# Moving more of an FFT and ReGLU kernel's mirror products from TensorE to GpSimd, with new buffers, 480 mirror columns and an fp32 row

## The chip, the cores and the metric

One core of a Trainium2 chip. The metric is the device time of one execution in microseconds (us); the profile's span is some 1.8 us shorter. Engines are named as in the profile: PE (TensorE matmul), PEld (its weight loads), DVE (VectorE), ACT (ScalarE), POOL (GpSimd), SP (SyncE, which here only issues DMAs). In a profile line, L465 is line 465 of the kernel that ran; the changed kernel has other line numbers.

## The reference

```python
X = np.fft.fft(x, axis=1)              # x: (8, 3008, 256)
X = np.fft.fft(X, axis=2)
y = X.real.reshape(24064, 256)
gate = np.maximum(y @ w_gate, 0.0)     # w_gate, w_val: (256, 1536)
val = y @ w_val
out = (gate * val) @ w_out             # w_out: (1536, 256)
```

The kernel folds the transform along the model axis into the weights. The real part of a 2D transform is symmetric: the output row k and its mirror row -k come from the same two arrays (called p and q in the kernel), once as gate = relu(P + Q), once as relu(P - Q); the value likewise.

## The kernel before

There are eight images. Each has three blocks of 12 steps, so there are 288 steps, numbered t; a step is one block and one of 12 slices of the hidden width. Each step makes an h tile of 128x2x512: half 0 is the direct product gate times value, half 1 the mirror product. A second matmul, 12 steps later, multiplies h by w_out.

PE's results go to PSUM (the memory that matmuls write and add into), bank by bank. Other intermediate tiles come from rings: a ring of five buffers gives a sixth tile no place until the first has been read for the last time.

The mirror's *value* can be had in two ways:

- **Not split:** PE adds a third matmul into the value's PSUM bank (with the weights wm, which are -2 times ws), and DVE multiplies it by the mirrored gate.
- **Split:** DVE keeps E (the even part: the value after its first matmul, plus a correction by the Nyquist row nb), later makes 2E - V of it, and POOL multiplies. PE is spared one matmul; DVE and POOL get more work.

```python
    gp = ctx.enter_context(tc.tile_pool(name="gp", bufs=5, space=SB))
    ep = ctx.enter_context(tc.tile_pool(name="ep", bufs=3, space=SB))
    op = ctx.enter_context(tc.tile_pool(name="op", bufs=3, space=SB))

    def split(t):
        return NBLK * NF + 8 <= t < len(steps) and t % 3 != 2      # from step 44 on

    def gate(t):
        ...                                          # two matmuls into G
        nc.scalar.activation(e["gs"][:], e["G"][:], ACTF.Relu)     # gs: a gp buffer

    def mirror_gate(t):
        nc.tensor.matmul(e["G"][:], lhsT=wm[0]..., rhs=pqt[b, blk][:, 1, :], start=False, ...)
        e["gm"] = gp.tile([128, 512], F32, tag="gs", name="gm")    # gm: the same ring as gs
        nc.scalar.activation(e["gm"][:], e["G"][:], ACTF.Relu)

    def even(t):
        e["E"] = ep.tile([128, 512], F32, tag="e", name="E")
        nc.vector.scalar_tensor_tensor(e["E"][:], nbt[b, blk][:], af[:, f:f + 1], e["V"][:],
                                       op0=ALU.mult, op1=ALU.add)

    def mirror_value(t):
        if split(t):
            nc.vector.scalar_tensor_tensor(e["E"][:], e["E"][:], 2.0, e["V"][:], op0=ALU.mult, op1=ALU.subtract)
            mirror_h(t, nc.gpsimd, e["E"])           # h half 1 = gm * E, on POOL
        else:
            nc.tensor.matmul(e["V"][:], lhsT=wm[1]..., rhs=pqt[b, blk][:, 1, :], start=False, ...)
            mirror_h(t, nc.vector, e["V"])
```

The PE order of a step matters: gate(t), then the *second* value matmul of step t-1 (value(t-1, 1)), then half of the output matmuls, then the first value matmul of step t and E of it on DVE. So the second value matmul of t-1 waits until DVE has read the bank for E(t-1).

POOL has a second duty. In 22 steps of an image it **folds** the input of the image after the next (sums and differences of rows, in place): one operation at the end of each step, behind that step's mirror product, on a queue that keeps its order.

```python
            at(t0 + tl, load_x, b + 2, nc.sync)                       # from image 2: step 7
            at(t0 + tf, lambda b=b: folds.append(fold(b + 2, nc.gpsimd)))  # from image 2: step 13
    ...
        for k in range(2 if t < NBLK * NF + 8 else 1):
            while folds and next(folds[0], folds) is folds:
                folds.pop(0)
```

One part of a fold's input (the tile xl) is loaded through SP, the other (xh) by an indirect DMA that POOL itself issues, from the same queue:

```python
    def load_x(b, q):
        ...                                          # xl: two DMAs on q, which is SP
        nc.gpsimd.indirect_dma_start(out=xh[:]..., ...)
```

Five folds (of images 3 to 7, run during images 1 to 5) fall where steps are split; the fold of image 2 ends there.

## Time and profile before

| | before |
|---|---|
| time, median | 690.5 us (690.15 to 691.46, 4 runs) |
| PE, DVE, ACT, POOL busy | 95%, 74%, 63%, 62% |
| matmul pitch, start to start | 0.215 us at 512 columns, 0.109 us at 256 |
| PE work of a steady image by these pitches | 76.1 us, of 79 to 80 us that it takes |
| one fold | 46.9 us for 22 steps |

The first part of the page of the kernel before (busy time of each engine), and from its second part the rows of PE and POOL in 40 equal slices of the span, in tenths:

```profile
PE 653.0 (95%) x4297; PEld 419.5 (61%) x4297; DVE 508.5 (74%) x800; ACT 436.2 (63%) x811; POOL 424.1 (62%) x398
...
PE   2799999999999999999999999999899999999996
...
POOL 1219801984998499747995399846996343344331
```

The share of POOL says little: 62% is a mean of stretches of 9 (folds) and of 3 to 5. The stretch view over one fold of the kernel before, with busy us and number of instructions by engine, shows it:

```profile
core 0: us, PE busy (x) PEld busy (x) DVE busy (x) ACT busy (x) POOL busy (x), PEclk, DMA share, GB/s
237.40:284.30 46.90, 44.81 (x308) 28.79 (x306) 36.58 (x57) 29.87 (x56) 46.74 (x43) 1.00 0.25 72
```

POOL is busy for 46.74 of 46.90 us. Inside, the timeline of POOL (start, duration, line, what it is) has no gap between the mirror products (L465) and the fold:

```profile
256.61 1.27 POOL L465 TENSOR_TENSOR h<-gm,E 128x512 bf16<-128x512 f32 x1
257.84 1.80 POOL L100 TENSOR_TENSOR xl<-xl,xh 94x768 f32<-94x768 f32 x1
259.61 1.26 POOL L465 TENSOR_TENSOR h<-gm,E 128x512 bf16<-128x512 f32 x1
260.84 0.98 POOL L101 TENSOR_TENSOR eo<-xc 94x381 bf16<-94x381 f32 x1
261.78 0.20 POOL L103 CAST eo<-xl 94x6 bf16<-94x6 f32 x1
261.93 0.98 POOL L104 TENSOR_TENSOR eo<-xl 94x381 bf16<-94x381 f32 x1
262.88 1.26 POOL L465 TENSOR_TENSOR h<-gm,E 128x512 bf16<-128x512 f32 x1
```

A mirror product takes 1.23 us of POOL's time (start to the next start), an operation of the fold 0.15 to 1.8. The waits view (who waited for whom: total us, times, longest) shows how that reaches PE. ACT's next gs wants a buffer of the shared ring that POOL's late product still reads, and PE's mirror-gate matmul (L439) waits for gs:

```profile
POOL h L465 <- DVE E L473: 166.0, 87, 3.8
...
ACT gs L434 <- POOL h L465: 12.6, 16, 1.2
...
PE G L439 <- ACT gs L434: 9.5, 14, 1.0
```

The first line is the other side: outside folds POOL sits idle, waiting for work.

### The profile page before, as it was taken

The page shows a single profiled execution, that of the slowest core. Times are in us where ns is not written, and L with a number is a line of the kernel's source. Part 1 is how long each engine was busy: PE and PEld are TensorE (multiplying, and loading weights), DVE is VectorE, ACT ScalarE, POOL GpSimd, SP SyncE. Part 2 cuts the span into 40 slices and gives each one's busy share as a digit, 9 for nine tenths or more (in the row PEclk, how much of TensorE's full clock was granted, in tenths as well). Part 3 has the DMA queues.
Part 4 walks back from the last instruction along what each step waited for, and adds up shares of the span by engine and source line. Part 5 has one row for each costly group of instructions (what it writes and reads, how often), then busy time and mean ns, then how long its engine had stood idle before and what let it go on. Part 6 is the DMA issues. An engine that isn't in the chain of part 4 may idle for free.

```text
span 688.8 us, 12467 instructions
## 1 busy us (share of the span) xinstructions
PE 653.0 (95%) x4297; PEld 419.5 (61%) x4297; DVE 508.5 (74%) x800; ACT 436.2 (63%) x811; POOL 424.1 (62%) x398
## 2 busy tenths in 40 slices
PE   2799999999999999999999999999899999999996
PEld 1444665666566656666666666666566666666665
DVE  8447555578778778787778878778788788888881
ACT  5555665667676766676666757676666856665561
POOL 1219801984998499747995399846996343344331
PEclk9999999999999999999999999999999999999999
DMA  9692257239314822176112931258211241211213
GB/s 235 216 218 37 63 143 173 48 97 203 113 50 122 199 79 74 40 167 203 38 42 67 234 105 41 74 124 216 59 48 38 60 123 38 78 32 36 54 31 90
DMA packets 31843, 70.74 MB, mean 103 GB/s; under 512 B 4410, under 2 KB 21426, under 8 KB 29394
## 3 DMA queue, kind: packets, MB, share of 16 engines
q1 hardware_dynamic: 29444, 58.16, 31.6%
q0 software_dynamic: 2336, 11.80, 8.4%
q8 instruction: 33, 0.54, 0.4%
q14 instruction: 30, 0.25, 0.1%
HBM read 39.77 MB, written 30.96 MB: 103 GB/s over the span
## 4 chain that ended last, share of the span: by engine, by line
PE 61%; POOL 18%; DMA 10%; issue 5%; DVE 2%; ACT 2%; SPq 1%; POOLq 0%; DVEq 0%
PE po L494 24%; PE V L451 7%; POOL h L465 7%; PE G L439 6%; PE G L432 6%; PE G L433 6%; PE V L449 6%; DMA xl<-in_x_dram 5%; POOL xl L100 4%; POOL xc L99 4%; PE V L476 3%; DMA xh<-in_x_dram,ix 3%; DMA xh<-in_x_dram 2%; PE psw L251 2%; POOL eo L101 2%
## 5 line engine op out<-in xcount | busy, mean ns | idle before, releaser
L494 PE MATMUL po<-wo,h 128*128 128x256 bf16 x2304 | 323.2, 272 | 0.0
L465 POOL TENSOR_TENSOR h<-gm,E 128x512 bf16<-128x512 f32 x162 | 205.9, 1271 | 166.6 <-DVE E L473 166.0
L494 PEld LDWEIGHTS <-h 128*128 128x128 bf16 x2304 | 222.8, 98 | 83.5 <-issue 7.5
L442 ACT ACTIVATE gm<-G 128x512 f32<-128x512 f32 x288 | 172.5, 599 | 129.8 <-PE G L439 128.2
L453 DVE TENSOR_TENSOR h<-gs,V 128x512 bf16<-128x512 f32 x288 | 190.7, 685 | 58.7 <-PE V L451 47.1
L434 ACT ACTIVATE gs<-G 128x512 f32<-128x512 f32 x288 | 171.6, 596 | 15.0 <-POOL h L465 12.6
L465 DVE TENSOR_TENSOR h<-gm,V 128x512 bf16<-128x512 f32 x126 | 86.7, 688 | 85.6 <-ACT gm L442 60.8
L459 DVE SCALAR_TENSOR_TENSOR E<-nb,af,V 128x512 f32<-128x512 bf16 x162 | 120.8, 746 | 6.6 <-PE V L449 6.1
L439 PE MATMUL G<-pq,wm_107 128*128 128x512 bf16 x288 | 109.1, 379 | 9.9 <-ACT gs L434 9.5
L473 DVE SCALAR_TENSOR_TENSOR E<-E,V 128x512 f32<-128x512 f32 x162 | 110.2, 680 | 0.0
L432 PE MATMUL G<-pq,wc_103 128*128 128x512 bf16 x288 | 109.1, 379 | 1.0 <-ACT pq L206 1.0
L449 PE MATMUL V<-pq,wc_104 128*128 128x512 bf16 x288 | 109.1, 379 | 0.0
L433 PE MATMUL G<-pq,ws_105 128*128 128x512 bf16 x288 | 109.1, 379 | 0.0
L451 PE MATMUL V<-pq,ws_106 128*128 128x512 bf16 x288 | 109.0, 379 | 0.0
L497 ACT COPY os<-po 128x512 f32<-128x512 f32 x96 | 56.2, 585 | 67.9 <-PE po L494 67.9
L99 POOL TENSOR_TENSOR xc<-xl,xh 94x768 f32<-94x768 f32 x35 | 63.4, 1811 | 50.0 <-DMA xl<-in_x_dram 34.1
L100 POOL TENSOR_TENSOR xl<-xl,xh 94x768 f32<-94x768 f32 x35 | 63.4, 1812 | 1.6
L433 PEld LDWEIGHTS <-ws_105 128*128 128x128 bf16 x288 | 28.1, 98 | 35.0 <-issue 1.1
L451 PEld LDWEIGHTS <-ws_106 128*128 128x128 bf16 x288 | 28.1, 98 | 34.2 <-DVE ws_106 L256 0.4
L476 PE MATMUL V<-pq,wm_108 128*128 128x512 bf16 x126 | 47.7, 379 | 0.3
L432 PEld LDWEIGHTS <-wc_103 128*128 128x128 bf16 x288 | 28.1, 98 | 18.6 <-issue 15.6
L449 PEld LDWEIGHTS <-wc_104 128*128 128x128 bf16 x288 | 28.2, 98 | 17.6 <-issue 1.3
(361 smaller groups left out, 385.5 us busy)
## 6 DMA issues: line engine op xcount, KB each, us to landing
out_dram<-os SPq DMA_DIRECT2D x176, 128.0 KB
xl<-in_x_dram SPq DMA_DIRECT2D x7, 1360.0 KB
nb<-Nd SPq DMA_DIRECT2D x24, 128.0 KB
xl<-in_x_dram SPq DMA_DIRECT2D x7, 238.0 KB
xl<-in_x_dram SPq DMA_DIRECT2D x2, 768.0 KB
xh<-in_x_dram SPq DMA_DIRECT2D x2, 768.0 KB
wst<-in_moe_w_gate_dram SPq DMA_DIRECT2D x6, 256.0 KB
wst<-in_moe_w_val_dram SPq DMA_DIRECT2D x6, 256.0 KB
```

What stands on the lines that cost most here:

```text
L432: nc.tensor.matmul(e["G"][:], lhsT=wc[0][:, fs], rhs=pq[:, 0, :], start=True, stop=False)
L433: nc.tensor.matmul(e["G"][:], lhsT=ws[0][:, fs], rhs=pq[:, 1, :], start=False, stop=True)
L434: nc.scalar.activation(e["gs"][:], e["G"][:], ACTF.Relu)
L439: nc.tensor.matmul(e["G"][:], lhsT=wm[0][:, f * 128:(f + 1) * 128], rhs=pqt[b, blk][:, 1, :], start=False, stop=True, skip_group_check=True)
L442: nc.scalar.activation(e["gm"][:], e["G"][:], ACTF.Relu)
L449: nc.tensor.matmul(e["V"][:], lhsT=wc[1][:, fs], rhs=pq[:, 0, :], start=True, stop=split(t))
L451: nc.tensor.matmul(e["V"][:], lhsT=ws[1][:, fs], rhs=pq[:, 1, :], start=False, stop=True, skip_group_check=split(t))
L453: nc.vector.tensor_tensor(e["h"][:, 0, :], e["gs"][:], e["V"][:], op=ALU.mult)
L459: nc.vector.scalar_tensor_tensor(e["E"][:], nbt[b, blk][:], af[:, f:f + 1], e["V"][:], op0=ALU.mult, op1=ALU.add)
L465: eng.tensor_tensor(free(e["h"][:], 512 + NB - 1, [NB, 16], [-1, NB]), e["gm"][:].rearrange("p (a k) -> p a k", k=NB), val[:].rearrange("p ...
L473: nc.vector.scalar_tensor_tensor(e["E"][:], e["E"][:], 2.0, e["V"][:], op0=ALU.mult, op1=ALU.subtract)
L494: nc.tensor.matmul(po[:, s % 2, :], lhsT=ht[t - f + ff]["h"][:, sg, g * 128:(g + 1) * 128], rhs=wo[:, ff, :], start=(ff == 0), stop=(ff == ...
```

## The change

The intent: spare PE 41 more value matmuls, give POOL more room to lag (gm gets its own four buffers, E four), and leave out 32 of 512 mirror columns in the first and last block, whose results are never stored (h is set to zero there). The Nyquist row is made fp32 by a copy on POOL before it is broadcast.

```diff
-    Nd = nc.dram_tensor("Nd", (B * NBLK, 512), BF16, kind="Internal").ap()
+    Nd = nc.dram_tensor("Nd", (B * NBLK, 512), F32, kind="Internal").ap()
@@ stage2
-            nbt[b, blk] = pqp.tile([128, 512], BF16, tag="nb", name="nb")
+            nbt[b, blk] = pqp.tile([128, 512], F32, tag="nb", name="nb")
-            nc.sync.dma_start(out=row, in_=pq[0:1, 1, :])
+            nr = pqp.tile([1, 512], F32, tag="nr", bufs=1, name="nr")
+            nc.gpsimd.tensor_copy(nr[:], pq[0:1, 1, :])
+            nc.sync.dma_start(out=row, in_=nr[:])
@@ pools
-    gp bufs=5   ep bufs=3   op bufs=3          (shortened)
+    gp bufs=2   ep bufs=4   op bufs=2
@@ steps
+    def mirrored(t):
+        blk = steps[t][1]
+        return slice(NB if blk == 0 else 0, 512 - NB if blk == NBLK - 1 else 512)
     def split(t):
-        return NBLK * NF + 8 <= t < len(steps) and t % 3 != 2
+        return NBLK * NF + 8 <= t < len(steps) and t % 6 != 5
@@ gate
+        cols = mirrored(t)
+        if cols.stop - cols.start < 512:
+            lo = 0 if cols.start else cols.stop
+            nc.gpsimd.memset(e["h"][:, 1, lo:lo + NB], 0.0)
@@ mirror_gate
-        e["gm"] = gp.tile([128, 512], F32, tag="gs", name="gm")
-        nc.scalar.activation(e["gm"][:], e["G"][:], ACTF.Relu)
+        e["gm"] = ep.tile([128, 512], F32, tag="gm", name="gm")
+        nc.scalar.activation(e["gm"][:, cols], e["G"][:, cols], ACTF.Relu)
... (the same [:, cols] in the mirror matmuls, E, 2E - V and the mirror products)
```

More of the change, by code (lines that the diff above doesn't have):

```diff
@@ L412 @@
     stage2(0, 0, 1, "dve")
-    gp = ctx.enter_context(tc.tile_pool(name="gp", bufs=5, space=SB))
-    ep = ctx.enter_context(tc.tile_pool(name="ep", bufs=3, space=SB))
-    op = ctx.enter_context(tc.tile_pool(name="op", bufs=3, space=SB))
+    gp = ctx.enter_context(tc.tile_pool(name="gp", bufs=2, space=SB))
+    ep = ctx.enter_context(tc.tile_pool(name="ep", bufs=4, space=SB))
+    op = ctx.enter_context(tc.tile_pool(name="op", bufs=2, space=SB))
     steps = [(b, blk, f) for b in range(B) for blk in range(NBLK) for f in range(NF)]
     ht = {}
+    def mirrored(t):
+        blk = steps[t][1]
+        return slice(NB if blk == 0 else 0, 512 - NB if blk == NBLK - 1 else 512)
     def split(t):
-        return NBLK * NF + 8 <= t < len(steps) and t % 3 != 2
+        return NBLK * NF + 8 <= t < len(steps) and t % 6 != 5
     def gate(t):
@@ L434, in gate @@
         nc.scalar.activation(e["gs"][:], e["G"][:], ACTF.Relu)
+        cols = mirrored(t)
+        if cols.stop - cols.start < 512:
+            lo = 0 if cols.start else cols.stop
+            nc.gpsimd.memset(e["h"][:, 1, lo:lo + NB], 0.0)
     def mirror_gate(t):
         b, blk, f = steps[t]
-        e = ht[t]
-        nc.tensor.matmul(e["G"][:], lhsT=wm[0][:, f * 128:(f + 1) * 128], rhs=pqt[b, blk][:, 1, :],
+        e, cols = ht[t], mirrored(t)
+        nc.tensor.matmul(e["G"][:, cols], lhsT=wm[0][:, f * 128:(f + 1) * 128], rhs=pqt[b, blk][:, 1, cols],
                          start=False, stop=True, skip_group_check=True)
-        e["gm"] = gp.tile([128, 512], F32, tag="gs", name="gm")
-        nc.scalar.activation(e["gm"][:], e["G"][:], ACTF.Relu)
+        e["gm"] = ep.tile([128, 512], F32, tag="gm", name="gm")
+        nc.scalar.activation(e["gm"][:, cols], e["G"][:, cols], ACTF.Relu)
     def value(t, part):
@@ L456, in even @@
         b, blk, f = steps[t]
-        e = ht[t]
+        e, cols = ht[t], mirrored(t)
         e["E"] = ep.tile([128, 512], F32, tag="e", name="E")
-        nc.vector.scalar_tensor_tensor(e["E"][:], nbt[b, blk][:], af[:, f:f + 1], e["V"][:],
+        nc.vector.scalar_tensor_tensor(e["E"][:, cols], nbt[b, blk][:, cols], af[:, f:f + 1], e["V"][:, cols],
                                        op0=ALU.mult, op1=ALU.add)
     def mirror_h(t, eng, val):
-        e = ht[t]
-        eng.tensor_tensor(free(e["h"][:], 512 + NB - 1, [NB, 16], [-1, NB]),
-                          e["gm"][:].rearrange("p (a k) -> p a k", k=NB),
-                          val[:].rearrange("p (a k) -> p a k", k=NB), op=ALU.mult)
+        e, cols = ht[t], mirrored(t)
+        eng.tensor_tensor(free(e["h"][:], 512 + cols.start + NB - 1, [NB, (cols.stop - cols.start) // NB], [-1, NB]),
+                          e["gm"][:, cols].rearrange("p (a k) -> p a k", k=NB),
+                          val[:, cols].rearrange("p (a k) -> p a k", k=NB), op=ALU.mult)
     def mirror_value(t):
         b, blk, f = steps[t]
-        e = ht[t]
+        e, cols = ht[t], mirrored(t)
         if split(t):
-            nc.vector.scalar_tensor_tensor(e["E"][:], e["E"][:], 2.0, e["V"][:], op0=ALU.mult, op1=ALU.subtract)
+            nc.vector.scalar_tensor_tensor(e["E"][:, cols], e["E"][:, cols], 2.0, e["V"][:, cols],
+                                           op0=ALU.mult, op1=ALU.subtract)
             mirror_h(t, nc.gpsimd, e["E"])
         else:
-            nc.tensor.matmul(e["V"][:], lhsT=wm[1][:, f * 128:(f + 1) * 128], rhs=pqt[b, blk][:, 1, :],
+            nc.tensor.matmul(e["V"][:, cols], lhsT=wm[1][:, f * 128:(f + 1) * 128], rhs=pqt[b, blk][:, 1, cols],
                              start=False, stop=True, skip_group_check=True)
```

## The prediction

> **What bounds it now.** The page gives PE 95% busy of 688.8 us, DVE 74%, ACT 63%, POOL 62%. In the timeline a 128x512 matmul starts 0.215 us after the one before it and a 128x256 one 0.109 us, and I cost PE work by these pitches. The Trainium skill, "TensorE: Matmul & The Clock Gate", section "Wait — 56ns, not 53.3ns?", has N/2.4 + 2.5 ns (215.7 ns at 512), which the trace confirms. By that ledger a steady image is 76.1 us of PE work and lasts 79-80 us; stalls inside the 288 steps sum to about 18 us. They are: 0.11 us after each non-split step (PE's V L451 waits for DVE E L459), and 0.7-1.1 us at a few steps while POOL folds (waits view: ACT gs <- POOL h 12.6 us in 16 waits, PE G L439 <- ACT gs 9.5 us). In a fold (237.4 to 285.5 us) POOL runs without a gap: 29.7 us of fold and 15 h products of 1.23 us pitch in 22 steps. So the folds are already bound by POOL, the rest by PE.
>
> **What the change removes.** Split steps go from 162 to 203: 41 mirror-value matmuls x 0.216 = 8.8 us of PE. 480 columns: 252 matmuls shorter by 13 ns = 3.4 us. PE total: -12.2 us. Half of the 0.11 us stalls go.
>
> **What it adds.** POOL: 41 more h. Fitting its fp32 two-input spans (991 ns at 381, 1811 at 768: 2.12 ns per element) gives 1.17 us pitch at 480. The skill's "GPSIMD Engine Reference", section "Performance versus the Vector engine", gives about 2.6 cycles per element for two inputs, and this agrees. 192 memsets, estimated 0.15 us (the 94x6 cast's pitch), and 24 row copies, estimated 0.6 us (about one cycle per element by that section, plus 0.19). DVE: 41 x about 0.7 us; an all-split step needs about 1.95 us on DVE against 1.95 on PE, balanced. nb in fp32 should leave E L459 at its 1x rate (about 0.71 us at 480).
>
> **On the critical path.** Own gm buffers and four E buffers let POOL lag about 3.7 us instead of 0.95 before something stalls (next binding wait: DVE E for its fourth-last split step's POOL h). But a 22-step fold now has POOL work of about 56 us against 45 us of PE. Net of the slack that leaves about 7.5 us of stall per fold (5 folds in the split region), against about 3 us now: +22 us. With -12.2 us of PE work: about +9, 699; shaded down because memset and row copy are guessed: **695 us**, range 680 to 707. Chances: faster by over 2% 0.07, within 2% 0.75, slower 0.18.
>
> **What would show it.** Mirror-value matmuls 85 (was 126). Waits: ACT gs <- POOL h gone; DVE E L459 (or ACT gm) <- POOL h new, tens of us, in fold windows. Images 6 and 7 (no folds, after about 525 us) faster by about 2 us each; images 1 to 5 each slower by 1-4 us. POOL total about 480 us. E at about 0.71 us.
>
> **What would make it wrong.** If memset and row copy are nearly free, or the lag allowed is larger, fold stalls shrink and the time falls to 680-685. If DVE's write of h must wait for POOL's memset of the same tile, or SP waits behind the row copy, or two os buffers are too few, it goes above 705.

## The result

The changed kernel takes 700.45 us (699.75 to 700.87, 4 runs) against 690.48: slower, ratio 1.0141 with a 95% interval of 1.0123 to 1.0159. A ratio here is the mean time of a kernel's fast runs over that of the other's of the same rounds, so it is not quite the ratio of the medians quoted. It lies within the two per cent that count as the same, but it is clear of the noise.

The same parts of the page after the change:

```profile
PE 639.4 (91%) x4179; PEld 415.7 (59%) x4256; DVE 529.6 (76%) x841; ACT 429.3 (61%) x811; POOL 491.1 (70%) x655
...
PE   2899999999988989899988998899988999999997
...
POOL 1219811996999599966999589975999555555451
```

PE has less to do and is less busy; the 8s in its row stand where POOL's row has 9s. (This trace lacks some matmul records: of 288 gate matmuls of one line it has 246. The weight loads are complete, so counts and step times below are taken from those.) One fold in the stretch view:

```profile
324.70:378.20 53.50, 47.67 (x323) 30.74 (x327) 41.86 (x67) 30.87 (x60) 53.38 (x61) 1.00 0.22 70
```

POOL is again busy throughout, and the fold now lasts 53.5 us. The timeline of POOL inside it shows what was added; L477 is the mirror product, L446 the memset, L213 the copy of the row:

```profile
352.74 0.12 POOL L446 MEMSET h<- 128x32 bf16 x1
352.80 0.60 POOL L213 CAST nr<-pq 1x512 f32<-1x512 bf16 x1
353.37 1.19 POOL L477 TENSOR_TENSOR h<-gm,E 128x480 bf16<-128x480 f32 x1
354.52 1.81 POOL L99 TENSOR_TENSOR xc<-xl,xh 94x768 f32<-94x768 f32 x1
356.28 0.11 POOL L446 MEMSET h<- 128x32 bf16 x1
356.36 1.19 POOL L477 TENSOR_TENSOR h<-gm,E 128x480 bf16<-128x480 f32 x1
```

Start to start, the memset takes 0.07 us, the row copy 0.57 and the product 1.15 at 480 columns. Four more products, eleven memsets and three row copies in a fold come to 4 x 1.2 + 11 x 0.07 + 3 x 0.57 = 7.3 us, less 0.7 for nine or ten products shortened by 0.08: 6.6 us, which is the growth from 46.9 to 53.5.

The waits view after. The wait for a shared gs buffer is gone, and new ones stand in its place:

```profile
ACT gm L454 <- POOL h L477: 60.8, 46, 2.3
...
PE V L463 <- DVE E L471: 19.9, 17, 2.0
...
DVE E L471 <- POOL h L477: 16.8, 12, 2.0
...
PE G L451 <- ACT gs L441: 10.8, 20, 1.2
```

How one such wait reaches PE can be read in the timeline of all engines. The idle time of the engine before an instruction, and who ended it, stand in brackets:

```profile
338.92 1.26 POOL L477 TENSOR_TENSOR h<-gm,E 128x512 bf16<-128x512 f32 x1
...
340.14 0.99 POOL L101 TENSOR_TENSOR eo<-xc 94x381 bf16<-94x381 f32 x1
340.21 0.60 ACT L454 ACTIVATE gm<-G 128x512 f32<-128x512 f32 x1 [1.77 <-POOL h L477]
340.22 0.75 DVE L471 SCALAR_TENSOR_TENSOR E<-nb,af,V 128x512 f32<-128x512 f32 x1 [1.33 <-POOL h L477]
...
341.02 0.38 PE L463 MATMUL V<-pq,ws_106 128*128 128x512 bf16 x1 [1.28 <-DVE E L471]
```

POOL ends an older product at 340.18. The gm and E rings hold four buffers each, and only then is one of each free; DVE writes E until 340.97; only then may PE add to that bank, at 341.02, after 1.28 us of idleness.

Where the 10 us came from is seen by image. The times are worked out from the traces, from the first gate weight load of an image to that of the next:

```
                 head   im0   im1   im2   im3   im4   im5   im6   im7   tail  (us)
before           33.1  89.8  80.4  79.8  79.6  78.7  79.6  76.9  72.1  18.8
after            33.9  88.7  82.1  86.8  81.3  80.9  81.6  75.4  69.8  18.4
```

Images 6 and 7, without a fold, gain 1.5 and 2.3 us. Images 1 to 5 lose 14.6 us together, 7.0 of them in image 2. There the step times (from the same weight loads) show two losses against image 3 of the changed kernel: 3.8 us in the first six steps, in which image 1's fold still runs, and 1.8 in steps 18 to 23, after a late start of image 2's own fold. The timelines of POOL show that start, before and then after: POOL's issue of the load of xh, and the fold's first operation, which waits for it:

```profile
218.76 0.96 POOL L85 DMA_INDIRECT xh<-in_x_dram,ix  x1 [0.16 <-issue]
237.40 1.81 POOL L99 TENSOR_TENSOR xc<-xl,xh 94x768 f32<-94x768 f32 x1 [0.68 <-DMA xh<-in_x_dram,ix]
```

```profile
226.73 0.97 POOL L85 DMA_INDIRECT xh<-in_x_dram,ix  x1 [0.16 <-issue]
243.51 1.82 POOL L99 TENSOR_TENSOR xc<-xl,xh 94x768 f32<-94x768 f32 x1 [2.96 <-DMA xh<-in_x_dram,ix]
```

The issue stands in POOL's queue behind image 1's fold, which ends at 217.37 before and at 225.23 after. So it comes 15.5 us after the start of image 2 before, and 22.1 us after it in the changed kernel, and POOL idles 3.0 us in place of 0.7 with mirror products queued behind. The lag of one fold delays the next.

### The profile page after: what moved, and what is told of

It reads as the page before. It is cut to its first block, busy times and chain, and to the rows that moved or that the text cites. A ratio compares the mean times of both kernels' runs of the same rounds, so it can differ in the third digit from the quotient of the medians.

```text
span 699.0 us, 12606 instructions
## 1 busy us (share of the span) xinstructions
PE 639.4 (91%) x4179; PEld 415.7 (59%) x4256; DVE 529.6 (76%) x841; ACT 429.3 (61%) x811; POOL 491.1 (70%) x655
## 4 chain that ended last, share of the span: by engine, by line
PE 64%; POOL 19%; issue 8%; DVE 4%; DMA 2%; ACT 1%; SPq 0%; POOLq 0%; DVEq 0%; ACTq 0%
PE po L507 25%; PE G L440 7%; PE V L463 7%; POOL h L477 6%; PE G L451 6%; PE V L461 6%; PE G L439 5%; POOL xc L99 4%; PE psw L253 3%; POOL xl L100 3%; PE V L489 2%; POOL eo L104 2%; POOL eo L101 2%; DVE E L471 2%; DMA xh<-in_x_dram 2%
## 5 line engine op out<-in xcount | busy, mean ns | idle before, releaser
L507 PE MATMUL po<-wo,h 128*128 128x256 bf16 x2304 | 329.9, 272 | 1.3
L477 POOL TENSOR_TENSOR h<-gm,E 128x480 bf16<-128x480 f32 (+1 forms) x203 | 248.7, 1225 | 104.4 <-DVE E L485 89.1
L454 ACT ACTIVATE gm<-G 128x480 f32<-128x480 f32 (+1 forms) x288 | 167.4, 581 | 164.7 <-PE G L451 92.2
L471 DVE SCALAR_TENSOR_TENSOR E<-nb,af,V 128x480 f32<-128x480 f32 (+1 forms) x203 | 147.0, 724 | 34.0 <-POOL h L477 16.8
L485 DVE SCALAR_TENSOR_TENSOR E<-E,V 128x480 f32<-128x480 f32 (+1 forms) x203 | 133.6, 658 | 0.0
L463 PE MATMUL V<-pq,ws_106 128*128 128x512 bf16 x281 | 106.3, 378 | 20.2 <-DVE E L471 19.9
L451 PE MATMUL G<-pq,wm_107 128*128 128x480 bf16 (+1 forms) x288 | 106.6, 370 | 11.3 <-ACT gs L441 10.8
L440 PE MATMUL G<-pq,ws_105 128*128 128x512 bf16 x283 | 107.2, 379 | 2.2
L477 DVE TENSOR_TENSOR h<-gm,V 128x480 bf16<-128x480 f32 (+1 forms) x85 | 56.5, 664 | 65.9 <-ACT gm L454 41.8
L461 PE MATMUL V<-pq,wc_104 128*128 128x512 bf16 x265 | 100.4, 379 | 0.0
L439 PE MATMUL G<-pq,wc_103 128*128 128x512 bf16 x246 | 93.2, 379 | 1.0 <-ACT pq L206 1.0
L99 POOL TENSOR_TENSOR xc<-xl,xh 94x768 f32<-94x768 f32 x35 | 63.4, 1811 | 21.2 <-DMA xh<-in_x_dram,ix 21.2
L100 POOL TENSOR_TENSOR xl<-xl,xh 94x768 f32<-94x768 f32 x35 | 63.4, 1811 | 1.2
L213 POOL CAST nr<-pq 1x512 f32<-1x512 bf16 x24 | 14.4, 600 | 30.3 <-issue 26.1
```

Of the source, the lines that this page charges most:

```text
L439: nc.tensor.matmul(e["G"][:], lhsT=wc[0][:, fs], rhs=pq[:, 0, :], start=True, stop=False)
L440: nc.tensor.matmul(e["G"][:], lhsT=ws[0][:, fs], rhs=pq[:, 1, :], start=False, stop=True)
L451: nc.tensor.matmul(e["G"][:, cols], lhsT=wm[0][:, f * 128:(f + 1) * 128], rhs=pqt[b, blk][:, 1, cols], start=False, stop=True, skip_group_ ...
L454: nc.scalar.activation(e["gm"][:, cols], e["G"][:, cols], ACTF.Relu)
L461: nc.tensor.matmul(e["V"][:], lhsT=wc[1][:, fs], rhs=pq[:, 0, :], start=True, stop=split(t))
L463: nc.tensor.matmul(e["V"][:], lhsT=ws[1][:, fs], rhs=pq[:, 1, :], start=False, stop=True, skip_group_check=split(t))
```

## The experiments

Four theories were set against each other.

1. POOL's queue is overfull while it folds; its lag reaches PE through the gm and E buffers.
2. The fp32 row and its way through POOL, SP and DRAM is the cost.
3. Two gs or two os buffers are too few.
4. DVE is the limit, since a step that is split needs about as long on DVE as on PE.

Each group of four ran on one chip beside the kernel before. All outputs are right. A common table stands at the end of the section.

### Each part undone, in the changed kernel

**u1_third**, two of three steps split again:

```diff
-        return NBLK * NF + 8 <= t < len(steps) and t % 6 != 5
+        return NBLK * NF + 8 <= t < len(steps) and t % 3 != 2
```

> The changed kernel with 4 of 6 steps split again (every third step not split), all else kept. Theory 1 (POOL is overfull while it folds; its lag reaches PE through the gm and E buffers): 15 instead of 19 h products per fold, so the lag fits the new buffers and fold stalls fall from about 6.7 to about 1 us per image, against +8.6 us of PE for 41 more mirror-value matmuls: 677 us (672 to 683), faster than the kernel before. Theory 2 (the fp32 row's way through POOL and SP is the cost) and theory 3 (two gs or two os buffers are too few): stalls stay, 705 us or more.

Measured: 679.98 us, ratio to the kernel before 0.9821 (0.9777 to 0.9864), within the range of theory 1. PE has 41 more matmuls than in the changed kernel, and the kernel is 20 us faster. Folds are 48.7 us long. Theories 2 and 3 alone cannot be the cause.

**u2_bf16row**, the row in bf16 again:

```diff
-            nc.gpsimd.tensor_copy(nr[:], pq[0:1, 1, :])
-            nc.sync.dma_start(out=row, in_=nr[:])
+            nc.sync.dma_start(out=row, in_=pq[0:1, 1, :])      # Nd and nb bf16
```

> The changed kernel with the Nyquist row in bf16 again, no copy on POOL. Theory 1: each fold loses two row copies of 0.57 us ahead of the step that binds, 5 folds: about -6 us, 695 us (692 to 697). Theory 2: the whole loss goes, 690 us or less. Theory 4 (DVE is the limit in all-split runs; E reads fp32): E L471's span stays 713 and 746 ns by theory 1, and gets longer or shorter by theory 4.

Measured: 691.49 us, ratio 0.9988 (0.9944 to 1.0032): 9 us less by the medians, where theory 1 had said 6 (692 to 697). Images 2 to 5 gain 1.2 to 1.5 us each, about as expected (two copies of 0.57 us ahead of the step that binds). The miss is image 1, which gains 4.0: in the changed kernel the fold of image 3 starts after POOL has waited 1.7 us for its input, here without a wait, and POOL's lag is 1.6 us smaller from the first step on. The traces say why. The input waited for is xh, which POOL loads itself, not SP. In the changed kernel the row copy stands in POOL's queue before the fold of image 2, which starts 1.5 us before image 1 does and here 3.2 us before it; that fold ends 31.4 us after the start of image 1, here 28.6, and the load of xh behind it is issued after 34.0 us, here 31.2 (29.0 in the kernel before). Some 1.3 of the 4.0 us are lost in step 49, where the fold of image 2 meets split steps, the rest in steps 65 to 71. E's span does not depend on the type of nb. The groups by shape, first of the changed kernel and then of this run (count, total us, mean ns, idle before):

```profile
L471 DVE SCALAR_TENSOR_TENSOR E<-nb,af,V 128x480 f32<-128x480 f32 x133 | 94.8, 713 | 25.3 <-POOL h L477 10.3 <-PE V L461 7.7 <-PE G L440 3.8
...
L471 DVE SCALAR_TENSOR_TENSOR E<-nb,af,V 128x512 f32<-128x512 f32 x70 | 52.2, 746 | 8.7 <-POOL h L477 6.5 <-PE V L461 1.9
```

```profile
L469 DVE SCALAR_TENSOR_TENSOR E<-nb,af,V 128x480 f32<-128x480 bf16 x133 | 94.9, 713 | 21.8 <-POOL h L475 11.4 <-PE V L459 8.0 <-POOL h L444 1.4
...
L469 DVE SCALAR_TENSOR_TENSOR E<-nb,af,V 128x512 f32<-128x512 bf16 x70 | 52.3, 747 | 7.5 <-POOL h L475 4.9 <-PE V L459 2.3
```

713 and 746 ns with fp32, 713 and 747 with bf16. The Trainium skill's page "VectorE: DVE Perf Modes", section "Why PSUM operands drop a tier", says that a PSUM operand caps an fp32 operation at one element per cycle; V is one here. 32 more columns take 33 ns more with either type of nb, which agrees; no run here had E without a PSUM operand.

**u3_full512**, all 512 mirror columns and no memsets:

```diff
-        return slice(NB if blk == 0 else 0, 512 - NB if blk == NBLK - 1 else 512)
+        return slice(0, 512)
```

> The changed kernel with all 512 mirror columns and no memsets. Theory 1: PE +3.4 us of matmul; on POOL in a fold, memsets of 0.07 us pitch go and h grows by 0.08, about even; so 703 us (701 to 706). If the memsets (a wait of POOL on old readers of h, or a wait of DVE on them) were a cost of their own: below 700.

Measured: 702.41 us, ratio 1.0153 (1.0108 to 1.0198). As expected, though on the edge of what can be told: its interval overlaps that of the change. By the medians the 480 columns are worth about 2 us, which is not clear of the noise, and no harm of the memsets' own is seen.

**u4_sharedring**, the buffers of before:

```diff
-    gp bufs=2   ep bufs=4   op bufs=2          (shortened)
+    gp bufs=5   ep bufs=3   op bufs=3
-        e["gm"] = ep.tile([128, 512], F32, tag="gm", name="gm")
+        e["gm"] = gp.tile([128, 512], F32, tag="gs", name="gm")
```

> The changed kernel with the buffers of before: gs and gm share a ring of five, three E, three os. Theory 1: allowed POOL lag falls from about 3.7 to about 1 us, so each of 5 folds stalls 2.7 us more: 714 us (708 to 720), with waits of ACT gs for POOL h back. Theory 3 (two gs or two os buffers too few): 698 us or less.

Measured: 719.91 us, ratio 1.0406 (1.0356 to 1.0455), at the upper edge of theory 1. So the new buffers are worth 18 us (by the ratios) to 19.5 (by the medians) in this kernel, and theory 3 falls. The waits of before are back, and larger:

```profile
ACT gs L441 <- POOL h L477: 66.9, 59, 5.9
...
PE G L451 <- ACT gs L441: 39.6, 42, 5.0
```

### One part alone, in the kernel before

**a1_sixth_only**:

```diff
-        return NBLK * NF + 8 <= t < len(steps) and t % 3 != 2
+        return NBLK * NF + 8 <= t < len(steps) and t % 6 != 5
```

> The kernel before with nothing but 5 of 6 steps split. Theory 1 (POOL's fold sets the length): a fold grows from 46.9 us by four h of 1.23 us to 51.8 us and the shared ring still lets POOL lag only 1 us, so 5 folds cost about +24 us, against -4.5 us of PE outside folds and -3 us of small stalls: 708 us (702 to 714). Theory 3 or 2 (buffers or fp32 row made the change slow): faster than before, about 680.

Measured: 706.18 us, ratio 1.0211 (1.0184 to 1.0239), within the range of theory 1; folds 51.8 us long, as worked out. The step that spares PE the most makes the kernel before 15 us slower by itself.

**a2_own_only**, the pools and gm's own buffers and nothing else (the reverse of the diff of u4_sharedring, in the kernel before):

> The kernel before with nothing but the buffers of the change (gm its own four, four E, two gs, two os). Theory 1: the same POOL work, but a lag of about 5 us is now allowed, so the 3 us of stall in each of 4 to 5 folds go: 678 us (674 to 683); folds still 46.9 us long. Theory 3 (two gs or two os are too few): no faster than before.

Measured: 681.34 us, ratio 0.9852 (0.9832 to 0.9873). The folds are as long as before (47.0 us), with the same work on every engine; only PE no longer waits for them. Its waits:

```profile
PE G L439 <- ACT gs L434: 2.5, 2, 1.6
ACT gm L442 <- POOL h L465: 2.4, 2, 1.3
```

So the change holds one part that is worth some 10 us alone (0.0148 of 691), and the other parts together gave away twice that.

### The same work at another time, and more work at two times

**s1_actrow**, the fp32 row copied by ACT:

```diff
-            nc.gpsimd.tensor_copy(nr[:], pq[0:1, 1, :])
+            nc.scalar.copy(nr[:], pq[0:1, 1, :])
```

> The changed kernel with the fp32 row copied by ACT in place of POOL. If the row's cost is POOL's time (and SP waiting for POOL): as with the bf16 row, 692 us (689 to 695). If it is fp32 itself (DVE reading fp32 nb, twice the broadcast bytes): 700 us.

Measured: 694.83 us, ratio 1.0040 (1.0013 to 1.0068). Most of the row's cost was POOL's time (and what followed from it); the median is some 3 us above that of the bf16 row, but the intervals overlap, and by image (table below, from the profiled executions) the two runs agree within 0.4 us in each of images 1 to 7. So a cost of fp32 itself, apart from POOL's time, is not shown.

**s2_spread**, the changed kernel with the same instructions, the fold handed to POOL more slowly:

```diff
-        for k in range(2 if t < NBLK * NF + 8 else 1):
+        rest = t >= 72 and t % 36 in (17, 22, 27, 32, 0)
+        for k in range(2 if t < NBLK * NF + 8 else 0 if rest else 1):
```

> The changed kernel with the same instructions, but from image 2 on the 22 fold operations are given to POOL in 27 steps in place of 22 (none in every fifth step). Theory 1: POOL's excess inside the fold falls from about 6.7 to about 2.4 us, in four images: 684 us (680 to 689). Theory 4 (DVE's all-split steps) and theory 2: unchanged, 700 us.

Measured: 686.11 us, ratio 0.9915 (0.9889 to 0.9941). No instruction was taken away, DVE has the same work, and 14 us are gone by the medians. Theory 4 falls as the main cause.

**d1_inside and d2_outside**, from the kernel with the bf16 row, forty useless POOL copies of 0.57 us:

```diff
+        if 72 <= t < 216 and t % 36 in range(15, 25):      # d2_outside: range(2, 12)
+            nc.gpsimd.tensor_copy(dum[:], one512[:])       # 1x512, bf16 to fp32; two small buffers of their own
```

> The changed kernel with the bf16 row (691.5 us in its earlier run) and ten useless POOL copies (0.57 us each) per image in steps 15 to 24 of images 2 to 5, inside the folds. Theory 1: all 4 x 5.7 us come out at the end: +23 us, 714 us (709 to 719). If only POOL's total mattered, it would cost the same as the run with the copies outside.

> The same forty useless POOL copies, in steps 2 to 11 of images 2 to 5, where no fold runs and POOL idles about 0.8 us a step. Theory 1: they fill idle time, +0 to +4 us: 693 us (691 to 696).

Measured: inside 713.16 us, ratio 1.0323 (1.0305 to 1.0342); outside 691.36 us, ratio 1.0000 (0.9982 to 1.0018). Their base, the kernel with the bf16 row, had the ratio 0.9988. So by ratios the 40 x 0.57 = 22.8 us of useless work cost 0.0335 x 691 = 23 us inside the folds, and 1 us outside, which is within the intervals. By image, only image 2 grew, by 1.0 us; its steps 2 to 8 still hold image 1's fold, so that these copies are not all outside. One thing more differs: PE's granted clock over images 2 to 5 was 0.98 inside and 1.00 outside. But each of these images grew by 4.8 to 5.9 us over the bf16 row's run, about the 5.7 us of its copies, so the clock is not needed to explain the 23 us. Their waits, first inside, then outside:

```profile
DVE E L472 <- POOL h L478: 29.5, 17, 2.8
PE V L464 <- DVE E L472: 25.7, 15, 2.8
```

```profile
DVE E L472 <- POOL h L478: 14.6, 13, 2.0
PE V L464 <- DVE E L472: 13.7, 16, 1.8
```

POOL's total work is the same in both. Only the place of it counts.

### Versions that beat both

**b2_spread5**: the bf16 row, the spread fold, and five gm and five E buffers.

```diff
-    ep = ctx.enter_context(tc.tile_pool(name="ep", bufs=4, space=SB))
+    ep = ctx.enter_context(tc.tile_pool(name="ep", bufs=5, space=SB))
```

> The changed kernel with the bf16 row, folds spread over 27 steps and five gm and five E buffers (one step more of allowed lag, about 2 us). Theory 1: the spread kernel's 686 us, less about 8 for the row, less about 1.5 us of remaining stall in each of 4 folds: 673 us (668 to 679).

Measured: 671.33 us, ratio 0.9721 (0.9697 to 0.9745).

**b3_spread_fold3**: the same, with the split made by what POOL is doing.

```diff
-        return NBLK * NF + 8 <= t < len(steps) and t % 6 != 5
+        return NBLK * NF + 8 <= t < len(steps) and t % (3 if 13 <= t % 36 and t < 216 else 6) != (2 if 13 <= t % 36 and t < 216 else 5)
```

> As the last, but two of three steps are split in steps 13 to 35 of images 1 to 5 (while a fold runs) and five of six elsewhere. Theory 1: POOL's fold now fits, stalls nearly gone, against 3 to 4 more mirror-value matmuls per image (+4 us of PE in all): 671 us (665 to 677), about even with the last.

Measured: 671.35 us, ratio 0.9716 (0.9700 to 0.9733). Even, as expected: what the one pays in rests of stall, the other pays in matmuls. PE's row of slices is without an 8 after the head:

```profile
PE 642.2 (96%) x4276; PEld 417.6 (62%) x4276; DVE 515.2 (77%) x821; ACT 428.3 (64%) x811; POOL 453.6 (68%) x611
...
PE   1899999999999999999999999999999999999996
```

### All runs by image

Times from the profiled execution of each; the head differs from run to run by some us.

```
                 head   im0   im1   im2   im3   im4   im5   im6   im7   tail   median  ratio
before           33.1  89.8  80.4  79.8  79.6  78.7  79.6  76.9  72.1  18.8   690.5   1
after            33.9  88.7  82.1  86.8  81.3  80.9  81.6  75.4  69.8  18.4   700.5   1.0141
u1_third         34.3  89.2  79.4  79.2  76.9  76.7  77.8  76.7  71.4  18.8   680.0   0.9821
u2_bf16row       37.0  88.9  78.1  85.3  79.8  79.5  80.4  75.4  69.8  18.5   691.5   0.9988
u3_full512       34.4  89.4  81.3  87.0  81.2  80.6  81.3  76.0  70.4  18.9   702.4   1.0153
u4_sharedring    34.9  89.6  90.5  86.6  84.4  84.1  84.4  75.5  69.8  18.4   719.9   1.0406
a1_sixth_only    33.7  89.5  83.3  84.6  83.0  82.7  82.7  75.9  70.4  18.5   706.2   1.0211
a2_own_only      32.3  91.2  80.1  76.9  76.9  76.9  76.9  76.9  72.3  18.8   681.3   0.9852
s1_actrow        33.8  91.9  78.5  85.5  79.8  79.6  80.0  75.7  69.9  18.5   694.8   1.0040
s2_spread        33.6  90.8  82.1  83.0  76.8  76.5  77.2  76.2  69.8  18.5   686.1   0.9915
d1_inside        33.7  88.8  78.1  90.6  85.0  85.4  85.2  75.4  69.8  18.5   713.2   1.0323
d2_outside       34.3  89.6  78.2  86.3  79.1  79.4  79.5  75.4  69.8  18.5   691.4   1.0000
b2_spread5       32.8  90.5  78.0  79.1  76.7  74.8  75.1  74.8  69.5  18.5   671.3   0.9721
b3_spread_fold3  33.4  89.2  79.2  75.9  76.2  75.9  76.1  74.8  69.5  18.5   671.4   0.9716
```

The variants with five of six steps split all have 69.5 to 70.4 us in image 7, where nothing folds; those with two of three have 71.4 to 72.3. The saving on PE is real, and the folds take it back.

## Why the prediction was wrong

The direction and the mechanism were right, the size was not: 695 us was predicted, +5 on the kernel before, and +10 was measured.

- **What bounds it: right.** A fold is a stretch bound by POOL (46.74 of 46.90 us busy). The runs with useless copies show it: 22.8 us more of POOL work cost 23 us inside the folds and about 1 outside.
- **PE's saving of 12.2 us: right where it could be seen.** 85 mirror-value matmuls were left, and images 6 and 7 gained 1.5 and 2.3 us, where "about 2 us each" was said.
- **The stall of the folds: right in the sum, partly by luck.** The ledger said +22 us of stall, 4.5 for each of five equal folds. In images 1 to 5 the time grew by 14.6 us while their PE work fell by some 8.1 us (by the pitches: 5 matmuls of 0.216 us and 0.37 us of shorter ones in image 1, 6 and 0.37 in each of the other four), so the stalls grew by about 22.7. The new waits were the ones named (E and gm for POOL's h). But images 3 to 5 stalled by only 3.4 to 3.9 us more each, and images 1 and 2 by 11.8 together, where the ledger had 9.
- **What the ledger left out: POOL's own load.** It treats every fold alike. In images 1 and 2 POOL issues the load of xh late, behind the fold before, and then waits 1.7 and 3.0 us for it (none and 0.7 in the kernel before); in images 3 to 5 the issue is on time (14.3 us after the start of the image, 14.8 before). Over the runs, image 2 is 5.5 to 7.2 us longer than image 3 in seven of the eight in which its load was issued 21.5 us or more after its start (2.4 in the eighth, b2_spread5, which has five buffers), and at most 2.3 us longer in the others, where that was under 19 us. Image 2 also holds the end of image 1's fold, and no run moved this load alone, so this part is read from traces and not tested.
- **The small costs on POOL.** The memset was put at 0.15 us and takes 0.07; the row copy at 0.6 and takes 0.57. A fold's POOL work was put at 56 us and is 53.5; POOL's total was put at about 480 us and is 491.
- **The step that failed: "699; shaded down because memset and row copy are guessed: 695".** Terms of a sum whose errors could go either way were taken as a reason to move the sum one way, by nearly half of its +9. The memset's estimate was indeed too high, by 11 x 0.08 = 0.9 us a fold. But the row copy's was right, and what the ledger left out went the other way and was as large: by the run with the bf16 row, the row costs 9 us in all, where two copies ahead of the binding step in each of five folds make 6; 4.0 of the 9 are lost in image 1, where POOL starts a fold with more lag. All in all, images 1 and 2 stalled by 2.8 us more than the ledger's 9. The sum of the ledger as it stood, 699, missed the measured time by 1.5 us, but it did so with three folds counted too high and the first two too low.
- **DVE's balance: right.** Outside folds the steps that are split take 1.95 us on PE, and spreading the fold, with the same DVE work, brought 14 us.

Still open: whether an fp32 row costs anything apart from POOL's time, and how much of the loss in images 1 and 2 is due to POOL's late loads.

## What to carry to other kernels

An engine with a share of 62% can be the bound of half the program: cut the share by stage before giving it more work, and put the work where it idles (the same 40 useless copies cost 23 us in one place and about 1 us in another). When a late engine holds buffers that an earlier one wants, more buffers can be worth more than fewer instructions: they gave 10 us here with no work removed, and spreading a burst over more steps gave 14 to 16. Where an engine issues the loads of its own next burst, look for these issues in its queue: they are late when it is late. When a ledger made of measured pitches says one number, put the doubt into the range and not into the number.

## What the Trainium skill lacked or had wrong

- "GPSIMD Engine Reference", section "Performance versus the Vector engine", has about 2.6 cycles per element for two inputs. The fp32 sums of 381 and 768 elements here (991 and 1811 ns) give 2.12 ns per element, which is 2.5 cycles at the 1.2 GHz that the page gives: it agrees. For a loop body of at most two operations it has 1.03 cycles per element; the 1x512 copy of 600 ns roughly fits that with some 0.19 us of fixed time (estimated from the 94x6 copy's 0.2 us), a fixed time for which that section has no figure.
- The same page has no figure for a small memset. 128x32 bf16 took 121 ns, and the next instruction started 0.07 us after its start: the span overstates what a short POOL instruction costs in a full queue.
- "VectorE: DVE Perf Modes" has no row for the operation with a scalar and two tensors in its table of modes. Here it took 746 ns with a per-partition scalar and 680 ns with a constant at 512 columns, and the same with bf16 as with fp32 for one source.
